# Attention with queries in blocks of 128, two heads sharing the last block, and half of the probabilities divided on GpSimd

## The chip, the cores and the metric

One Trainium2 chip, one of its cores. The time is the device time of one execution in microseconds; 853.25 us is the median of three runs of the kernel before. Engine names as in the profile: PE is TensorE's matmul, PEld its weight load, DVE is VectorE, ACT is ScalarE, POOL is GpSimd, SP is the engine that issues the transfers.

## What is computed

```python
def _attn_ref(q, k, v, g_q, g_k):            # 4 batches, 12 heads, 448 tokens, 64 wide
    q_n, k_n = (rmsnorm(q, g_q), rmsnorm(k, g_k))
    scores = scale * np.matmul(q_n, k_n.transpose(0, 1, 3, 2))
    scores = scores - np.max(scores, axis=-1, keepdims=True)
    attn = np.exp(scores)
    attn = attn / (np.sum(attn, axis=-1, keepdims=True) + 1e-09)
    return np.matmul(attn, v)
```

The result goes, as 1792 tokens of 768, through a gated MLP (`silu(x @ w_gate) * (x @ w_val) @ w_out`, width 1536), and that through a soft mixture of 8 experts with 4 slots each: logits by `phi`, a softmax over the tokens that makes the slots' inputs, two matmuls per expert with a ReLU between, and a softmax over the slots that mixes their outputs. All is fp32.

## The kernel before, in words

The work is one program with a list of steps written out by hand. A step `t` handles one block of 112 queries of one **pair** of heads; there are 24 pairs (6 per batch, `i` in the code) and 4 blocks per pair (`c`). Matmuls with fp32r operands are made exact enough by splitting an operand into a high and a low part.

- **Stage 0** (`step0`, steps 0 to 27, order lists `ORD0` and `ORDB`): attention of batch 0 and the start of batch 1, beside the conversion of the MLP's weights from 64-bit words and the product of `w_out` and `phi`.
- **Later steps** (`step`): each step also does one unit `u` of the gated MLP, `gv` (line 596), in two halves `G0` and `G1` of nine matmuls each (line 607). Attention of batch b+1 runs beside the MLP of batch b. `ORD1` (line 1244) is the order of a step while the weights are still converted (`u` < 24), `ORD2` (line 1247) the one after. Attention ends at step 95, near 610 us; the rest of the MLP, the slots and the experts follow, and the experts' weights are loaded as buffers come free.

Each name in an order list is a part of the step, issued in that order; each engine executes its instructions in that order, and waits where an operand or a buffer is late. The parts of attention, in the order of the data:

- `T`, `TH`, `L` (`transp` 365, `transp_hi` 390, `transp_lo` 410): transpose q or k of the next pair, then make the high and low parts. For pairs 0 to 6 (`SPL = 7`) both heads stand in the two halves of the partitions, one instruction per part. For later pairs each head's high and low parts are stacked: `qa[:, j]` holds the high part of head j in its own half of the partitions and the low part in the other half, and k's high part is copied into both halves, by ACT or DVE, so a full-height matmul covers two of the three terms.
- `S` (`scores` 448): pairs 0 to 6 take three terms x two heads, each a matmul with 64 contraction rows (line 463); later pairs take four matmuls of 128 rows (466 and 468).
- `M0`, `M1` (`smax` 471, DVE) and `E0`, `E1` (`sexp` 477, ACT): maximum and exponential of each head, with the row sums in `su`.
- `P0`, `P1` (`ptrans` 513, PE) and `V0`, `V1` (`pevac` 524, ACT or DVE), one step later: transpose the probabilities and copy them out of PSUM.
- `NA`, `NB`, `NC` (`sums_inv` 488, `sums_spread` 499, `sums_evac` 509): invert the eight columns of sums, widen them to 64 columns each on POOL (`rs`, line 494), transpose that on PE (`rb`, line 504) and copy it out, so that the sums lie along the queries.
- `X` (`pv` 538): 16 matmuls on v for the whole pair, into the PSUM tile `xp`; `XM` (`pv_scale` 567, DVE) multiplies by the inverse sums; `XH`, `XL` (`split_hi` 583, `split_lo` 587) make the parts of x.
- `Q` (`norm_part` 357): squares on ACT, and on POOL the power (line 341) and the products (347) of the RMS norm of a later pair.

PSUM: all transposes, `xp` and the small results share three buffers of one tag (`pt_tile`, line 67); the scores rotate over three more.

Of the kernel before, what the change touches and what calls it, by code (L numbers as in the profile page):

```python
# [8 lines left out]
F32 = mybir.dt.float32  # L9
# [12 lines left out]
def attn_moe_softmoe_kernel(  # L22
# [366 lines left out]

    def transp_hi(i, n):  # L390

        if i >= NPR:
            return
        tq = st[i]["qk"[n]]
        qa, ka, kl = qk_tiles(i)
        if i < SPL:
            if n == 0:
                nc.scalar.activation(out=qa[:, 0], in_=tq[:, :S], func=AF.Copy, scale=gsc[:, 0:1])
            else:
                (nc.vector.tensor_copy if i < NP and HID else nc.scalar.copy)(out=ka[:, 0], in_=tq[:, :S])  # L400
            return
        for j, r in enumerate(halves):
            if n == 0:
                nc.scalar.activation(out=qa[r, j], in_=tq[r, :S], func=AF.Copy, scale=gsc[r, 0:1])
            else:
                nc.scalar.copy(out=ka[r, j], in_=tq[r, :S])
                if (KC0 if i < NP else KC1)[j] == "a":
                    nc.scalar.copy(out=ka[halves[1 - j], j], in_=tq[r, :S])

    def transp_lo(i, n):  # L410

        if i >= NPR:
            return
        tq = st[i].pop("qk"[n])
        qa, ka, kl = qk_tiles(i)
        if i < SPL:
            if n == 0:
                nc.vector.scalar_tensor_tensor(
                    out=qa[:, 1],
                    in0=tq[:, :S],  # L420
                    scalar=gsc[:, 0:1],
                    in1=qa[:, 0].bitcast(F32),
                    op0=ALU.mult,
                    op1=ALU.subtract,
                )
            else:
                sub_lo(kl[:, 0], tq[:, :S], ka[:, 0])
            return
        for j, r in enumerate(halves):
            if n == 1 and i < SPL + 2:  # L430
                nc.gpsimd.memset(kl.bitcast(F32)[halves[1 - j], j], 0.0)
            o = halves[1 - j]
            if n == 0:
                nc.vector.scalar_tensor_tensor(  # L434
                    out=qa[o, j],
                    in0=tq[r, :S],
                    scalar=gsc[r, 0:1],
                    in1=qa[r, j].bitcast(F32),
                    op0=ALU.mult,
                    op1=ALU.subtract,  # L440
                )
            else:
                sub_lo(kl[r, j], tq[r, :S], ka[r, j])
                kc = (KC0 if i < NP else KC1)[j]
                if kc != "a":
                    (nc.gpsimd if kc == "p" else nc.vector).tensor_copy(out=ka[o, j], in_=ka[r, j])

    def scores(t):

        i, c = divmod(t, NC)  # L450
        d = st[i]
        qa, ka, kl = qk_tiles(i)
        if t < M0 and t % 2:
            sc = [ps.tile([P, S], F32, tag=g, name="s")[:CP] for g in "gv"]
        elif t < M0:
            sc = [s_tile(j)[:CP] for j in range(2)]
        else:
            sc = [s_tile((2 * (t - M0) + j) % 3)[:CP] for j in range(2)]
        cs = slice(c * CP, (c + 1) * CP)
        if i < SPL:  # L460
# [3 lines left out]
        else:  # L464
# [4 lines left out]
        d[c] = {"sc": sc, "sm": ap_.tile([CP, 2], F32, tag="sm", name="sm", bufs=4), "pr": {}}  # L469

    def smax(t, j):
        d = st[t // NC][t % NC]
# [4 lines left out]
    def sexp(t, j):  # L477
        i, c = divmod(t, NC)
        d = st[i][c]
        if "su" not in st[i]:  # L480
            st[i]["su"] = ap_.tile([CP, NC, 2], F32, tag="su", name="su", bufs=3)
        p = ap_.tile([CP, S], F32, tag="pr", name="pr", bufs=PRB)
# [3 lines left out]
        d["pr"][j] = p  # L486

    def sums_inv(i):

        su = st[i]["su"].rearrange("p c j -> p (c j)")  # L490
        nc.scalar.activation(out=su, in_=su, func=AF.Copy, bias=EPS_SUM)
        nc.vector.reciprocal(out=su, in_=su)  # L492
        rs = ap_.tile([P, 2 * NC * HD], F32, tag="rs", name="rs", bufs=1)
        nc.gpsimd.tensor_copy(  # L494
            out=rs[:CP].rearrange("p (n d) -> p n d", d=HD), in_=su.unsqueeze(2).to_broadcast([CP, 2 * NC, HD])
        )
        st[i]["rs"] = rs

    def sums_spread(i):

        rs = st[i]["rs"][:CP].rearrange("p (c n) -> p c n", c=NC)
        rb = pt_tile("rb")
        for c in range(NC):
            nc.tensor.transpose(
                rb[:, c * CP : (c + 1) * CP], rs[:, c], ident[:CP, :CP]
            )
        st[i]["rb"] = rb

    def sums_evac(i):
        st[i]["rs"] = st[i]["rs"][:, :S]  # L510
        nc.scalar.copy(out=st[i]["rs"], in_=st[i].pop("rb")[:, :S])

    def ptrans(t, j):

        i, c = divmod(t, NC)
        pr = st[i][c]["pr"][j]
        tp = pt_tile("tp")
        for ck in range(NC):
            nc.tensor.transpose(  # L519
                tp[:CP, ck * CP : (ck + 1) * CP], pr[:, ck * CP : (ck + 1) * CP], ident[:CP, :CP]  # L520
            )
        st[i][c]["tp", j] = tp

    def pevac(t, j):
        i, c = divmod(t, NC)
        if c == 0:
            if i < NP and i % 2:
                pt = hnp.tile([CP, NC, 512], F32, tag="hn", name="pt", bufs=3)[:, :, :S]
            else:
                pt = ap_.tile([CP, NC, S], F32, tag="pt", name="pt", bufs=PTB)  # L530
            st[i].setdefault("pt", {})[j] = pt
        eng = nc.vector.tensor_copy if t < M0 and (t % 4, j) in PVD else nc.scalar.copy
        eng(  # L533
            out=st[i]["pt"][j][:, :, c * CP : (c + 1) * CP],
            in_=st[i][c]["tp", j][:CP, :S].rearrange("p (k q) -> p k q", k=NC),
        )
# [98 lines left out]

    def h_trans(u, ht=None):

        b, r = divmod(u, NU)
        fc = r // 2
        g, f4 = divmod(fc, 4)  # L640
        d = bt[b]
        if f4 == 0:
            d["hn"][g] = hnp.tile([CP, NC, 512], F32, tag="hn", name="hn", bufs=3)
        ht = d["ht"][fc] if ht is None else ht
# [3 lines left out]
        nc.scalar.copy(  # L648
            out=d["hn"][g][:, :, P * f4 : P * f4 + P], in_=th4[:CP, :].rearrange("p (c f) -> p c f", c=NC)
        )  # L650
# [407 lines left out]
    def step(t):  # L1058
# [114 lines left out]

        def P_(j):
# [48 lines left out]
        def Q_():  # L1223
# [6 lines left out]
            SP=SP, R0=R0, R=R_, CT=CT, C=C_, SS=SS, HT=HT, LG=LG, Q=Q_,  # L1230
# [14 lines left out]
        "SP X NB T S AT W4 NC XM TH XH M1 M0 Z1 P1 Z2 WH AM G0 Z3 P0 E1 XL L NA R0 CT V0 V1 SS WL G1 E0 Q HT Z4 LG R C"  # L1245
# [9 lines left out]
    KC0, KC1 = 'aa', 'va'  # L1255
# [9 lines left out]
        "X TP WT P0 M1 NB M0 NA TH WV R SS TL S V0 U2 NC U W2 XM CT P1 C G2 WE V1 XH XL E0 Q E1"  # L1265
# [228 lines left out]
```

## Time and profile before

| what | value |
|---|---|
| median of three runs | 853.25 us (852.73 to 855.25) |
| the profiled execution | 852.55 us, of which the span from first to last instruction is 850.2 us |
| mean granted TensorE clock | 0.977 |
| busy: PE, DVE, ACT, POOL | 801.2, 492.1, 487.2, 270.0 us |
| DMA | 148.87 MB, mean 175 GB/s |
| chain that ended last, by engine | PE 76%, DVE 8%, DMA 7%, POOL 3%, ACT 3%, issue 2% |

A row of a group of instructions names the line, the engine, the operation, what it writes and from what (`out<-in`), the shapes, and the count. The chain follows the work that ended last back from the end, at each step to what released it. A wait row says who waited for whom, how long in all, how often and the longest.

### The profile page before, as it was taken

Reading aid. Unit: us, or ns where it says so; the run is one execution under the profiler, and the core shown is the slowest. Engines: PE = TensorE matmul, PEld = TensorE weight load, DVE = VectorE, ACT = ScalarE, POOL = GpSimd, SP = SyncE. Lnnn points to the kernel's source line nnn. Section 1 sums busy time; section 2 is a strip of 40 time slices with the busy share of each in tenths; the row PEclk is TensorE's granted clock in tenths of the full one; section 3 lists DMA queues with packets and bytes.
Section 4 is the critical chain, followed back from the end, with each engine's and each line's share of the span. In section 5 each row is a group of like instructions: output and inputs, shape, how many; then the busy total and the mean of one; then the engine's idle time right before and its main releaser. Section 6 shows DMA issues by size and latency. Waiting matters only on the chain.

```text
span 850.2 us, 14278 instructions
## 1 busy us (share of the span) xinstructions
PE 801.2 (94%) x5504; PEld 612.8 (72%) x5504; DVE 492.1 (58%) x785; ACT 487.2 (57%) x1054; POOL 270.0 (32%) x211
## 2 busy tenths in 40 slices
PE   6899989999999999999999999999999999988685
PEld 5566657878877767788778678877888888655343
DVE  4899888889888556565646655554354434221013
ACT  4777877889877746676667467664532323211012
POOL 7977748676777023113330230200000000010000
PEclk8999999999999999999999999999999999999877
DMA  7666655576564322322132122221227888799997
GB/s 212 201 178 205 205 179 185 178 248 198 186 196 152 108 60 66 107 89 89 51 94 89 49 78 67 86 67 57 59 77 239 294 293 319 271 383 403 403 350 235
DMA packets 77891, 148.87 MB, mean 175 GB/s; under 512 B 5888, under 2 KB 48128, under 8 KB 77824
## 3 DMA queue, kind: packets, MB, share of 16 engines
q1 hardware_dynamic: 77824, 147.97, 52.5%
q8 instruction: 43, 0.70, 0.3%
q14 instruction: 24, 0.20, 0.1%
HBM read 128.29 MB, written 19.66 MB: 174 GB/s over the span
## 4 chain that ended last, share of the span: by engine, by line
PE 76%; DVE 8%; DMA 7%; POOL 3%; ACT 3%; issue 2%; SPq 0%; POOLq 0%; ACTq 0%; DVEq 0%
PE pg L607 36%; PE tp L519 7%; PE xp L547 6%; DMA w<-in_moe_w_dram 6%; PE s L466 3%; PE s L468 3%; PE th L647 2%; PE tq L372 2%; DVE sm L473 2%; PE s L547 2%; DVE qa L434 2%; PE so L1436 2%; PE s L463 2%; PE lp L668 2%; POOL rs L494 2%
## 5 line engine op out<-in xcount | busy, mean ns | idle before, releaser
L607 PE MATMUL pg<-xh,wh 128*128 128x448 f32 x576 | 219.6, 381 | 0.0
L607 PE MATMUL pg<-xl,wh 128*128 128x448 f32 x576 | 210.3, 365 | 0.0
L607 PE MATMUL pg<-xh,wl 128*128 128x448 f32 x432 | 158.1, 366 | 0.7 <-DVE wl L239 0.7
L473 DVE TENSOR_REDUCE sm<-s 112x1 f32<-112x448 f32 x192 | 110.7, 618 | 66.6 <-PE s L468 65.3
L483 ACT ACTIVATE pr<-s,sm 112x448 f32<-112x448 f32 x192 | 121.1, 635 | 37.5 <-DVE sm L473 36.3
L494 POOL COPY rs<-su 112x512 f32<-112x512 f32 x24 | 35.6, 1484 | 275.1 <-DVE su L492 268.2
L607 PEld LDWEIGHTS pg<-xh,wh 128*128 128x128 f32 x576 | 108.4, 188 | 17.9 <-issue 10.2
L607 PEld LDWEIGHTS pg<-xl,wh 128*128 128x128 f32 x576 | 108.6, 189 | 7.0
L519 PE MATMUL tp<-ident,pr 112*112 112x112 f32 x768 | 99.6, 261 | 3.0 <-ACT wot L253 1.1
L519 PEld LDWEIGHTS tp<-ident,pr 112*112 112x112 f32 x768 | 82.2, 134 | 17.9 <-issue 2.1
L231 ACT CAST wh<-raw 128x768 fp32r<-128x768 f32 x96 | 79.7, 831 | 25.2 <-PE pg L607 21.8
L533 ACT COPY pt<-tp 112x448 f32<-112x448 f32 x164 | 81.0, 539 | 13.8 <-PE tp L519 7.8
L607 PEld LDWEIGHTS pg<-xh,wl 128*128 128x128 f32 x432 | 81.1, 188 | 8.5 <-DVE wl L239 2.0
L239 DVE TENSOR_TENSOR wl<-raw,wh 128x768 fp32r<-128x768 f32 x72 | 72.7, 1009 | 23.4 <-ACT wh L231 23.1
L341 POOL TENSOR_TENSOR ri<-ss,mhalf 112x16 f32<-112x16 f32 (+1 forms) x25 | 70.2, 2806 | 2.1
L347 POOL TENSOR_TENSOR qn<-qk,ri 112x512 f32<-112x512 f32 x46 | 62.1, 1361 | 2.3
L621 ACT ACTIVATE ht<-pg 128x448 f32<-128x448 f32 x48 | 25.9, 539 | 56.3 <-PE pg L607 56.3
L547 PE MATMUL xp<-pt,vt 112*64 112x448 f32 x288 | 58.1, 545 | 0.0
L648 ACT COPY hn<-th 112x512 f32<-112x512 f32 x48 | 28.4, 592 | 46.6 <-PE th L647 45.2
L607 PE MATMUL pg<-xh,raw 128*128 128x448 f32 x144 | 52.7, 366 | 0.0
L197 POOL TENSOR_SCALAR hpos<-r 128x768 uint16<-128x768 int16 x36 | 44.6, 1239 | 12.2 <-DVE raw L212 8.8
L628 DVE SCALAR_TENSOR_TENSOR ht<-ht,pg 128x448 f32<-128x448 f32 x48 | 29.5, 614 | 31.9 <-ACT ht L621 31.3
(160 smaller groups left out, 1208.7 us busy)
## 6 DMA issues: line engine op xcount, KB each, us to landing
w<-in_moe_w_dram SPq DMA_DIRECT2D x25, 1536.0 KB, 10.3
raw<-w SPq DMA_DIRECT2D x72, 384.0 KB, 3.1
w<-raw SPq DMA_DIRECT2D x36, 384.0 KB, 3.0
r<-in_moe_w_out_dram SPq DMA_DIRECT2D x12, 768.0 KB, 5.2
r<-in_moe_w_gate_dram SPq DMA_DIRECT2D x12, 768.0 KB, 5.7
r<-in_moe_w_val_dram SPq DMA_DIRECT2D x12, 768.0 KB, 5.3
qk<-in_q_dram SPq DMA_DIRECT2D x24, 224.0 KB, 3.4
qk<-in_k_dram SPq DMA_DIRECT2D x24, 224.0 KB, 3.5
```

The costliest lines, as they stand in the source:

```text
L197: (nc.gpsimd if e == "p" else nc.vector).tensor_scalar(out=o, in0=src, scalar1=-float((0x3800, 0xB800)[j]), scalar2=8.0, op0=ALU.add, op1= ...
L231: (nc.vector.tensor_copy if u - NO < NU and WH1 == "v" else nc.scalar.copy)(out=wh, in_=wst[u]["raw"])
L239: eng.tensor_tensor(out=wl, in0=wst[u]["raw"], in1=wst[u]["wh"].bitcast(F32), op=ALU.subtract)
L341: nc.gpsimd.tensor_tensor(out=ri, in0=ss, in1=mhalf[:, : len(ns)], op=ALU.pow)
L347: eng.tensor_tensor(out=st[i]["qn"][:, n].rearrange("p c h d -> p h c d"), in0=st[i]["qk"][:, n], in1=st[i]["ri"][:, n] .rearrange("p (h c ...
L473: nc.vector.tensor_reduce(out=d["sm"][:, j : j + 1], in_=d["sc"][j], axis=AX.X, op=ALU.max, negate=True)
L483: nc.scalar.activation(out=p, in_=d["sc"][j], func=AF.Exp, bias=d["sm"][:, j : j + 1], accum_out=st[i]["su"][:, c, j : j + 1])
L494: nc.gpsimd.tensor_copy(out=rs[:CP].rearrange("p (n d) -> p n d", d=HD), in_=su.unsqueeze(2).to_broadcast([CP, 2 * NC, HD]))
L519: nc.tensor.transpose(tp[:CP, ck * CP : (ck + 1) * CP], pr[:, ck * CP : (ck + 1) * CP], ident[:CP, :CP])
L533: eng(out=st[i]["pt"][j][:, :, c * CP : (c + 1) * CP], in_=st[i][c]["tp", j][:CP, :S].rearrange("p (k q) -> p k q", k=NC),)
L547: nc.tensor.matmul(xp[HD * j : HD * j + HD, :S], d["vt"][:, j, ck, :], d["pt"][j][:, ck, :], start=(ck == 0), stop=(ck == NC - 1),)
L607: nc.tensor.matmul(d[r], wt[:, P * c : P * c + P], mv, start=(c == 0 and n == 0), stop=(c == KD - 1 and n == 2),)
```

## The change

Queries are cut into three blocks of 128 and one of 64 per head. The last 64 queries of both heads of a pair share one block: a tile `qz`, zeroed once, holds head 0's 64 queries in its half of the partitions and columns 0 to 63, head 1's in the other half and columns 64 to 127, so one full-height matmul gives the scores of both. All pairs now use the three-term form of the scores; the stacked form and its copies of k go. In batches 2 and 3 (pairs 12 to 23) the probabilities are divided by their sums on POOL before they are transposed, so the spreading of the sums and the multiplication of the output go there; the split of x reads PSUM. Blocks per pair stay four, the last with one tile of scores instead of two. The three order lists are rearranged.

```diff
+    QL = S % P
+    qz = [ap_.tile([P, 2, 2 * QL], F32R, name=f"qz{n}") for n in range(2)]
...
     def transp_lo(i, n):
...
+            for j, r in enumerate(halves):
+                nc.gpsimd.tensor_copy(out=qz[i % 2][r, :, QL * j : QL * j + QL], in_=qa[r, :, S - QL :])
+        else:
+            sub_lo(ka[:, 1], tq[:, :S], ka[:, 0])
...
     def scores(t):
-        if i < SPL:
-            for n, (wt, mv) in enumerate(((qa[:, 0], ka[:, 0]), (qa[:, 0], kl[:, 0]), (qa[:, 1], ka[:, 0]))):
+        terms = ((0, 0), (0, 1), (1, 0))
+        for n, (wt, mv) in enumerate(terms):
+            if c < NC - 1:
                 for j, r in enumerate(halves):
-                    nc.tensor.matmul(sc[j], wt[r, cs], mv[r, :], start=(n == 0), stop=(n == 2))
-        else:
-            for j in range(2):
-                nc.tensor.matmul(sc[j], qa[:, j, cs], ka[:, j], start=True, stop=False)
-            for j in range(2):
-                nc.tensor.matmul(sc[j], qa[:, j, cs], kl[:, j], start=False, stop=True)
+                    nc.tensor.matmul(
+                        sc[j], qa[r, wt, c * P : (c + 1) * P], ka[r, mv, :], start=(n == 0), stop=(n == 2)
+                    )
+            else:
+                nc.tensor.matmul(sc[0], qz[i % 2][:, wt], ka[:, mv], start=(n == 0), stop=(n == 2))
...
+    def normp(t, part):
+        i, c = divmod(t, NC)
+        if part > both(t):
+            return
+        su = st[i]["su"][:, c, : both(t)]
+        if part == 0:
+            nc.vector.tensor_scalar(out=su, in0=su, scalar1=EPS_SUM, scalar2=None, op0=ALU.add)
+            nc.vector.reciprocal(out=su, in_=su)
+        else:
+            j = part - 1
+            p = st[i][c]["pr"][j]
+            nc.gpsimd.tensor_scalar(out=p, in0=p, scalar1=su[:, j : j + 1], scalar2=1.0, op0=ALU.mult, op1=ALU.mult)
...
     def pevac(t, j):
...
+        if c < NC - 1:
+            eng(out=st[i]["pt"][j][:, :, c * P : (c + 1) * P], in_=tp)
+        else:
+            eng(out=st[i]["pt"][j][:, :, c * P :], in_=tp[:, :, QL * j : QL * j + QL])
...
     def pv_scale(i):
+        if i >= NPX:
+            xt[b, hp] = d["xp"][:, :S]
...
-        "AT NB X NC T S XM TH XH M0 M1 AM XL E0 E1 SP W4 G0 L NA Z1 Z3 WH P0 V0 P1 V1 Z2 Z4 HT LG SS R0 CT C WL G1 R Q"
+        "T S AT TH M0 Z3 NB X NC P0 AM XM XH W4 M1 XL SP CT E0 SS NA G0 E1 Z1 WH V0 N0 Z4 P1 Q HT L R0 N2 V1 N1 C Z2 WL R G1 LG"
```

`both(t)` is 1 for the last block of a pair and 2 otherwise. `NPX` is 12. `N0` is the sum and reciprocal, `N1` and `N2` are the multiplications of heads 0 and 1.

## Rows read from the trace of the kernel before

**Rows 1.** The page, part 1: busy time, share of the span, instructions.

```profile
PE 801.2 (94%) x5504; PEld 612.8 (72%) x5504; DVE 492.1 (58%) x785; ACT 487.2 (57%) x1054; POOL 270.0 (32%) x211
```

**Rows 2.** Stretches: length, busy time per engine (instructions), PE clock, DMA share, GB/s.

```profile
145.00:238.00 93.00, 93.00 (x558) 76.82 (x557) 78.97 (x109) 80.30 (x160) 65.64 (x39) 1.00 0.67 210
...
270.00:330.00 60.00, 56.95 (x341) 43.85 (x340) 37.04 (x58) 35.86 (x80) 13.10 (x10) 1.00 0.24 76
...
500.00:610.00 110.00, 108.84 (x640) 89.48 (x640) 56.74 (x91) 67.15 (x152) 16.36 (x13) 1.00 0.22 68
...
770.00:790.00 20.00, 17.30 (x346) 11.09 (x342) 0.77 (x6) 1.15 (x3) 0.94 (x3) 1.00 1.03 402
```

**Rows 3.** Chain of waits, one pair of batch 2: start, length, what.

```profile
530.24 0.39 PE rb L504 x4
530.63 3.16 PE xp L547 x16
...
542.23 0.77 PE tp L519 x8
543.00 0.44 PE th L647 x4
...
545.27 0.40 PE s L466 x2
545.67 0.40 PE s L468 x2
546.07 1.85 PE pg L607 x9
...
554.80 0.62 PE th L647 x4
...
557.25 0.39 PE rb L504 x4
```

**Rows 4.** Timeline of PE, one step of stage 0: start, length, what.

```profile
74.04 0.55 PE L519 MATMUL tp<-ident,pr 112*112 112x112 f32 x4
74.52 0.46 PE L463 MATMUL s<-ka,qa 64*112 64x448 f32 x2
74.81 0.36 PE L463 MATMUL s<-kl,qa 64*112 64x448 f32 x2
75.02 0.37 PE L463 MATMUL s<-ka,qa 64*112 64x448 f32 x2
75.31 0.41 PE L274 MATMUL wpq<-stack,wot 128*128 128x32 f32 x2
```

**Rows 5.** Waits of PE: for whom, us in total, times, longest.

```profile
PE th L647 <- DVE qa L434: 4.7, 10, 0.5
...
PE rb L504 <- POOL rs L494: 2.1, 1, 2.1
```

**Rows 6.** Timeline of ACT, one exponential of batch 2.

```profile
541.51 0.63 ACT L483 ACTIVATE pr<-s,sm 112x448 f32<-112x448 f32 x1
542.03 0.20 ACT L483 ACTIVATION_READ_ACCUMULATOR pr<-s,sm 112x1 f32 x1
```

**Rows 7.** Timeline of DVE in batch 2.

```profile
540.23 1.16 DVE L473 TENSOR_REDUCE sm<-s 112x1 f32<-112x448 f32 x2 [0.47 <-PE s L468]
541.30 0.61 DVE L634 SCALAR_TENSOR_TENSOR ht<-ht,pg 128x448 f32<-128x448 f32 x1
542.99 0.96 DVE L239 TENSOR_TENSOR wl<-raw,wh 128x768 fp32r<-128x768 f32 x1 [1.07 <-ACT wh L231]
...
554.68 0.20 DVE L492 RECIPROCAL su<-su 112x8 f32<-112x8 f32 x1
```

**Rows 8.** Timeline of POOL in batch 2.

```profile
499.61 2.29 POOL L494 COPY rs<-su 112x512 f32<-112x512 f32 x1 [25.04 <-DVE su L492]
...
502.27 2.90 POOL L341 TENSOR_TENSOR ri<-ss,mhalf 112x16 f32<-112x16 f32 x1
...
526.92 0.61 POOL L494 COPY rs<-su 112x512 f32<-112x512 f32 x1 [19.62 <-DVE su L492]
```

More of the change, by code (lines that the diff above doesn't have):

```diff
@@ L375, in transp, with qz_zeros @@
         st[i][nm] = tq
-    SPL = 7
+    NPX = 2 * NP
     halves = [slice(0, HD), slice(HD, P)]
-    klz = [ap_.tile([P, 2, S], F32R, name=f"kl{n}") for n in range(2)]
+    QL = S % P
+    qz = [ap_.tile([P, 2, 2 * QL], F32R, name=f"qz{n}") for n in range(2)]
+    def qz_zeros():
+        for n in range(2):
+            nc.vector.memset(qz[n].bitcast(F32), 0.0)
     def qk_tiles(i):
@@ L394, in transp_hi @@
         tq = st[i]["qk"[n]]
-        qa, ka, kl = qk_tiles(i)
-        if i < SPL:
-            if n == 0:
-                nc.scalar.activation(out=qa[:, 0], in_=tq[:, :S], func=AF.Copy, scale=gsc[:, 0:1])
-            else:
[L400 to L408, printed above, removed]
+        qa, ka = qk_tiles(i)
+        if n == 0:
+            nc.scalar.activation(out=qa[:, 0], in_=tq[:, :S], func=AF.Copy, scale=gsc[:, 0:1])
+        else:
+            (nc.vector.tensor_copy if i < NP and HID else nc.scalar.copy)(out=ka[:, 0], in_=tq[:, :S])
     def transp_lo(i, n):
@@ L414, in transp_lo @@
         tq = st[i].pop("qk"[n])
[L415 to L446, printed above, removed]
+        qa, ka = qk_tiles(i)
+        if n == 0:
+            nc.vector.scalar_tensor_tensor(
+                out=qa[:, 1],
+                in0=tq[:, :S],
+                scalar=gsc[:, 0:1],
+                in1=qa[:, 0].bitcast(F32),
+                op0=ALU.mult,
+                op1=ALU.subtract,
+            )
[3 more added lines that the diff above has]
+            sub_lo(ka[:, 1], tq[:, :S], ka[:, 0])
     def scores(t):
@@ L477, in sexp @@
     def sexp(t, j):
+        if j >= both(t):
+            return
         i, c = divmod(t, NC)
@@ L499, in sums_spread @@
     def sums_spread(i):
-        rs = st[i]["rs"][:CP].rearrange("p (c n) -> p c n", c=NC)
         rb = pt_tile("rb")
         for c in range(NC):
-            nc.tensor.transpose(
-                rb[:, c * CP : (c + 1) * CP], rs[:, c], ident[:CP, :CP]
-            )
+            cs = slice(c * P, (c + 1) * P)
+            nc.tensor.transpose(rb[:, cs], st[i]["rs"][:, cs], ident)
         st[i]["rb"] = rb
     def sums_evac(i):
-        st[i]["rs"] = st[i]["rs"][:, :S]
-        nc.scalar.copy(out=st[i]["rs"], in_=st[i].pop("rb")[:, :S])
+        rs = st[i]["rs"] = st[i]["rs"][:, :S]
+        rb = st[i].pop("rb")
+        n = S - QL
+        nc.scalar.copy(out=rs[:, :n], in_=rb[:, :n])
+        for j, r in enumerate(halves):
+            nc.scalar.copy(out=rs[r, n:], in_=rb[r, n + QL * j : n + QL * j + QL])
     def ptrans(t, j):
+        if j >= both(t):
+            return
         i, c = divmod(t, NC)
@@ L518, in ptrans @@
         for ck in range(NC):
[L519 to L521 removed]
+            nc.tensor.transpose(tp[:CP, ck * P : (ck + 1) * P], pr[:, ck * CP : (ck + 1) * CP], ident)
         st[i][c]["tp", j] = tp
@@ L570, in pv_scale @@
         d = st.pop(i)
+        if i >= NPX:
+            xt[b, hp] = d["xp"][:, :S]
+            if b == 3 and hp > 3:
+                xf = xfp.tile([P, S], F32, tag=f"xh{hp - 4}", name="xf", bufs=1)
+                nc.scalar.copy(out=xf, in_=xt[b, hp])
+                xt[b, hp] = xf
+            return
         if b == 3 and hp > 3:
@@ L647, in h_trans @@
             nc.tensor.transpose(th4[:CP, P * c : P * c + P], ht[:, CP * c : CP * c + CP], ident)
-        nc.scalar.copy(
-            out=d["hn"][g][:, :, P * f4 : P * f4 + P], in_=th4[:CP, :].rearrange("p (c f) -> p c f", c=NC)
-        )
+        nc.scalar.copy(out=hn[:, :, o : o + P], in_=th4[:CP, :].rearrange("p (c f) -> p c f", c=NC))
     def logits(u):
@@ L1172, in E_, with NP_ @@
                 sexp(t, j)
+        def NP_(part):
+            if att and i >= NPX:
+                normp(t, part)
         def P_(j):
@@ L1273, in attn_moe_softmoe_kernel @@
         setup()
+        qz_zeros()
         fill(16)
```

68 lines of the change are left out of this document (36 added, 32 removed).

## The prediction

> **What bounds the kernel now.** I read the busy shares first: TensorE (PE) is busy 94% of the span, VectorE and ScalarE under 60% [rows 1]. Shares mix stages, so the stretches come next [rows 2]. From 145 to 238 us, where attention of batch 1 runs beside the MoE of batch 0, PE is busy all 93 us. From 500 to 610 us, where attention of batches 2 and 3 runs beside the MoE of batches 1 and 2, it misses 1.2 of 110 us. It misses 3.05 us in 270 to 330. In the tail (770 to 790 us) PE is busy 17.3 of 20 us, but the DMA share is full at 402 GB/s: the expert weights bound it. Those loads are issued by steps and as buffers come free, so the tail starts earlier by as much as PE ends the stages before it earlier. A microsecond of PE's queue before 610 us is therefore a microsecond of the kernel; one of ScalarE or VectorE is worth what PE waits for it.
>
> The chain of waits shows one pair of heads in that stage, as pieces one after the other with no gap [rows 3]: from one group rb (530.24) to the next (557.25) is 27.01 us. Per block of queries it holds the scores, 0.40 + 0.41 us, and eight transposes of probabilities, 0.77 us; per pair once rb, 0.39 us, and the 16 matmuls on v, 3.16 us.
>
> **The change, part by part.** Pairs 0 to 6 have K=64 scores now, 7 to 23 stacked ones; pairs 12 to 23 lose the spreading of the sums.
>
> *Scores, blocks 0 to 2.* Pairs 7 to 23 go from four full-height matmuls (0.81 us) to six of half height. Pairs 0 to 6 show what those cost [rows 4]: the two halves run at once, since the groups of two start 0.20 to 0.30 us apart; from the transposes at 74.04 to the group behind at 75.31 is 1.27 us. Less four transposes (0.77 / 8 each, 0.385) that is 0.885 us, more than three times 0.20, the rest being lost at the two changes of shape. So +0.075 us x 3 blocks x 17 pairs = +3.8 us. Bounds: 0.61 us (no loss at the changes, -10.2 us) to 1.16 us (twice the loss, +17.9).
>
> *Scores, fourth block.* Both heads share three full-height matmuls, 0.61 us by 0.81 / 4: -0.20 x 17 = -3.4 us, and against 0.885 us in pairs 0 to 6, -0.27 x 7 = -1.9 us.
>
> *Transposes of probabilities.* 32 of 112 columns become 28 of 128. Four of 112 take 0.385 us, four of 128 take 0.44 us (th) [rows 3]: 8 x 0.385 = 3.08 against 7 x 0.44 = 3.08 us. Nothing. Pairs 0 to 11 still spread their sums, now with 128 columns: 12 x 0.05 = +0.6 us.
>
> *Sums of batches 2 and 3.* rb goes: 12 x 0.39 = -4.7 us. Its copy on ScalarE, the wide copy on GpSimd and the multiplication of the output go too; PE hid them, so nothing, except that PE waited once for the GpSimd copy, 2.1 us [rows 5]: -2.1 us.
>
> *A wait that goes.* PE waited ten times, 4.7 us in all, before th for VectorE's qa [rows 5]; the row at 554.80 is one, th drawn out to 0.62 us behind it [rows 3]. Two low parts of q, one per head, hold a PSUM slot of the three that all transposes share. The new code has one instruction there, and in that step the block before is a fourth one with a single group of transposes, so a slot is free: -4.7 us. Next late would be the second group of transposes in the step of the output, which needs the slot of xp or of the first group.
>
> *Division on GpSimd.* Per block it adds two small VectorE instructions and one or two GpSimd multiplications of 128x448 between the exponential and PE's transposes, one step later. The trace of before has no such multiplication. Lower bound: GpSimd's copy of 512 columns at 0.61 us [rows 8] scaled to 448, 0.53 us. Upper bound: the same copy at 2.29 us, when something held it. I take 0.6, as a one-input pass over SBUF is nearest to the copy. The tightest place is block 2. From its scores' start: scores 0.885; two maxima and the activation's product between them, 1.16 + 0.61 [rows 7], to 2.65; last exponential and its accumulator read, 0.63 + 0.20 [rows 6], to 3.5; sum and reciprocal at 0.20 each [rows 7], to 3.9; two multiplications to 5.1 us. PE comes to the first transpose after 0.885 + 0.44 + 1.85 + 0.44 + 0.44 + 1.85 + 0.61 = 6.5 us. 1.4 us are spare. After block 1 PE has the 3.16 us on v too, but the exponentials now stand behind the split of x; about 1.6 us are spare. After block 0 the next step's matmuls on v cover it; block 3 has one multiplication. Before its multiplications GpSimd has the power, 2.90 us once per pair [rows 8], which fits since rb's copy is gone. Cost nothing; without that cover two multiplications cost their excess over 2.6 us, 12 times each in two places.
>
> The Trainium skill speaks against this placement: GPSIMD Engine Reference, section Engine selection, gives elementwise work to VectorE, GpSimd being about twice slower with two inputs and near line rate with one. Twice VectorE's 0.61 us [rows 7] would be an estimate of 1.2 us each, the chain then ends at 6.3 us, and the sum stays; it leaves 0.2 us of cover. No row here shows this operation.
>
> *The rest.* ScalarE and VectorE lose an exponential, a maximum and the doubled copies of k per pair; that work was hidden, but some of the 3.05 us in 270 to 330 [rows 2] are waits for it: -1 us taken, 0 to -3 the bounds. The zeroing of two tiles at the start, two small GpSimd copies per pair and two more ScalarE copies in pairs 0 to 11 are small beside idle time: nothing; uncovered they would cost about a microsecond. Reordered lists move instructions inside a step, not PE's sum; if they uncover a wait, that is the first rival.
>
> Sum: +3.8 - 3.4 - 1.9 + 0.6 - 4.7 - 2.1 - 4.7 - 1 = -13.4 us. The profiled execution took 852.55 us (span 850.2), 0.7 below the median 853.25: 839.1 for it, 839.8 for a median; I write 839.5.
>
> **Rivals.**
>
> *A, the waits only move.* xp now stays in PSUM until both halves of x are split from it, in a step where three other groups want the three slots. For it: one wait of this sort exists, 0.47 us a time. Against: PE has 1.85 us of MoE before it needs the slot. Then the 4.7 + 2.1 + 1 us stay: 853.25 - 5.6 = 847.5.
>
> *B, GpSimd ends on the path, slower.* The place is the first transpose after blocks 1 and 2; it decides from 1.3 us per multiplication, and the kernel is slower than before from about 1.7. For it: the same copy took 0.61 and 2.29 us, and VectorE's wl of 0.96 us [rows 7] stands beside the multiplications in each step. At 2.0 us each, 1.4 + 1.2 us per pair are lost, 12 x 2.6 = 31: 870. Against: 1.4 us spare, and one wl can add 0.96 to the pair only once. The lock behind this is told in the Trainium skill, SBUF — State Buffer, section SBUF: two separate sides: GpSimd and a VectorE instruction with two SBUF inputs exclude each other for a whole instruction. The two durations of the copy fit it.
>
> *C, half-height scores cost more between MoE groups.* At the upper bound, 1.16 us, they cost +17.9 instead of +3.8: 853.5, no change. For it: nobody ran them in that stage. Against: the neighbours in rows 4 change shape just as often.
>
> **How the numbers follow.** Forecast 0.57, A 0.20, B 0.13, C 0.10. The range reaches down to 831 (scores at 0.70 us, all of the idle time gone) and up to 852, taking in A and part of C; B lies outside. About 0.3% (2.6 us) is what a measurement can tell from no change. Faster: forecast, A and the mild end of B, 0.80; same 0.09; slower 0.11.
>
> **What would show it.** Right: X to X about 26 us in batch 2; no rb after batch 1; PE's wait for qa gone; half-height scores near 0.885 us in the MoE stage; GpSimd's multiplications near 0.6 us with no PE wait on them; the tail as long as before. Wrong: PE waiting for GpSimd's pr, multiplications over 1.3 us, score groups over 1.1 us, or new waits in 100 to 330 us, where ScalarE and VectorE are fullest.

## The result, and the profile after

The kernel after takes 839.3 us (median of 4 runs, 838.59 to 839.75), the kernel before 853.92 in the runs beside it (852.73 to 855.25): ratio 0.9836, 95% interval 0.9813 to 0.9859. The prediction said 839.5. The total is right; two of its parts are wrong, by 8.3 and 6.3 us, in opposite directions.

The page, part 1 (busy time, share of the span, instructions) and two of its costliest groups, of the kernel after:

```profile
span 837.7 us, 14201 instructions
PE 794.4 (95%) x5424; PEld 596.0 (71%) x5424; DVE 464.6 (55%) x796; ACT 440.9 (53%) x957; POOL 333.1 (40%) x327
...
L486 POOL TENSOR_SCALAR pr<-pr,su 128x448 f32<-128x448 f32 x84 | 70.2, 847 | 117.3 <-DVE su L482 106.3
...
L423 POOL CAST qz<-qa 64x128 fp32r<-64x128 f32 x48 | 33.7, 703 | 83.4 <-DVE qa L414 75.1
```

The span is 12.5 us shorter than before [rows 1]. To see where, I set both traces on the same marks: the group of 16 matmuls on v (xp; "X" below), once per pair, from pair 6 on. X of pair 6 stands at 129.27 before and at 136.08 after; X of pair 22 at 584.83 and at 573.83.

- **Up to the first X: 6.8 us lost.** The prediction had about 1.5 gained there (1.9 less some of the 0.6 for rb).
- **From X of pair 6 to X of pair 22: 455.56 becomes 437.75, 17.8 us gained.** The prediction's terms for these 16 pairs make 11.5.
- **From there to the end: 265.4 becomes 263.9**, about what the last pair gains.

The stretches between these two X of the kernel before, cut at the pairs with the longer steps, two of the six with the sum of all (columns as in [rows 2]):

```profile
129.27:273.18 143.91, 141.13 (x835) 115.21 (x834) 120.51 (x167) 119.41 (x236) 104.72 (x63) 1.00 0.62 196
...
330.36:469.05 138.69, 136.10 (x805) 111.59 (x804) 80.81 (x128) 93.41 (x205) 33.43 (x25) 1.00 0.27 82
...
sum 455.56, PE 444.68 PEld 359.19 DVE 300.11 ACT 320.52 POOL 169.38; mean PE 74.11 PEld 59.86 DVE 50.02 ACT 53.42 POOL 28.23
```

The same stretches of the kernel after:

```profile
136.08:278.21 142.13, 141.50 (x843) 112.03 (x842) 107.35 (x155) 107.36 (x222) 96.11 (x70) 1.00 0.62 199
...
331.19:463.98 132.79, 132.79 (x791) 104.43 (x789) 76.11 (x138) 79.64 (x170) 61.45 (x68) 1.00 0.28 88
...
sum 437.75, PE 437.11 PEld 340.86 DVE 275.55 ACT 279.15 POOL 221.17; mean PE 72.85 PEld 56.81 DVE 45.92 ACT 46.53 POOL 36.86
```

PE was idle for 455.56 - 444.68 = 10.9 us between the marks before, and is idle for 0.6 after; its busy time fell by 7.6. So 10.2 us of the 17.8 are waits and 7.6 are work.

The chain of waits of the kernel after, from X of pair 20 to X of pair 21 (start, length, what), answers to [rows 3]:

```profile
521.75 3.16 PE xp L552 x16
524.90 0.58 PE tp L525 x4
525.48 1.84 PE pg L619 x9
...
529.59 0.81 PE s L442 x5
530.40 0.58 PE tp L525 x4
530.98 1.84 PE pg L619 x9
532.83 0.44 PE tp L525 x4
533.26 0.44 PE th L663 x4
...
535.52 0.60 PE s L446 x3
536.12 0.44 PE tp L525 x4
...
546.94 0.80 PE s L442 x6
547.74 3.16 PE xp L552 x16
```

X to X is 25.99 us, against 27.00 for the same two pairs before; the other pairs from 13 to 22 gain 1.0 to 1.4 us each, the one with longer steps (18 to 19) 2.75. A half-height block takes 0.80 or 0.81 us, as the full-height one did, and the transposes right behind take 0.58 instead of 0.44; where the matmuls on v stand right behind (547.74), nothing is added. The fourth block takes 0.60. There is no rb and no idle time.

The wait before th is gone, and one more look at the step of the fourth block's transposes shows why (PE, VectorE and ScalarE of the kernel after):

```profile
544.12 0.60 PE L663 MATMUL th<-ident,ht 128*112 128x128 f32 x4
544.73 0.67 DVE L414 SCALAR_TENSOR_TENSOR qa<-tq,gsc,qa 128x448 fp32r<-128x448 f32 x1
545.03 0.37 ACT L541 COPY pt<-tp 112x256 f32<-112x256 f32 x1
```

th starts before VectorE reads q's transpose (tq) for its low part and before ScalarE copies the block's one group of transposes (tp), so it has a slot that neither of them holds.

Three losses at the start show in PE's timeline (in brackets the idle time before, and for whom), of the kernel after:

```profile
18.44 1.01 PE L372 MATMUL tq<-ident,qn 112*128 112x112 f32 x4 [4.63 <-POOL qn L347]
...
44.17 0.88 PE L506 MATMUL rb<-ident,rs 128*128 128x128 f32 x4 [1.74 <-POOL rs L496]
44.97 1.49 PE L442 MATMUL s<-ka,qa 64*128 64x448 f32 x6
...
113.14 0.87 PE L247 MATMUL tw<-ident,raw 128*128 128x128 f32 x3 [2.67 <-DVE raw L212]
```

Before, the first of these waits took 2.18 us and the other two weren't there. For the first, POOL's own timeline, of the kernel before:

```profile
11.96 0.21 POOL L340 TENSOR_SCALAR ss<-ss 112x16 f32<-112x16 f32 x1 [2.45 <-DVE ss L327]
```

and of the kernel after:

```profile
13.34 0.64 POOL L423 CAST qz<-qa 64x128 fp32r<-64x128 f32 x2 [3.97 <-DVE qa L414]
14.07 0.21 POOL L340 TENSOR_SCALAR ss<-ss 112x16 f32<-112x16 f32 x1
```

The two small copies of pair 0's last columns of q take 0.64 us, but they wait until 13.34 for VectorE's low part of q, and the normalization of pair 1 stands behind them in POOL's queue: 2.1 us late. PE waits for it.

For the third, VectorE's timeline of the kernel after:

```profile
111.70 0.42 DVE L541 COPY pt<-tp 112x256 f32<-112x256 f32 x1 [2.00 <-ACT pt L541]
```

This is the copy of head 1's half of the fourth block, out of the one tile of transposes that both heads share. It waits 2.00 us until ScalarE has copied head 0's half, which stands in ScalarE's queue behind a pass of 1.19 us over the weights; raw, which PE waits for, stands behind it in VectorE's queue. That the shared tile makes one copy wait for the other is read from the code, not tested.

### The profile page after: what moved, and what is told of

The parts are those of the page before. It is cut to its first block, busy times and chain, and to the rows that moved or that the text cites. A ratio compares the mean times of both kernels' runs of the same rounds, so it can differ in the third digit from the quotient of the medians.

```text
span 837.7 us, 14201 instructions
## 1 busy us (share of the span) xinstructions
PE 794.4 (95%) x5424; PEld 596.0 (71%) x5424; DVE 464.6 (55%) x796; ACT 440.9 (53%) x957; POOL 333.1 (40%) x327
## 4 chain that ended last, share of the span: by engine, by line
PE 61%; DMA 4%; ACT 1%; DVE 1%; POOL 1%; SPq 0%; issue 0%; DVEq 0%; ACTq 0%; POOLq 0%
PE pg L619 33%; PE tp L525 5%; PE xp L552 5%; DMA w<-in_moe_w_dram 4%; PE s L442 3%; PE so L1456 3%; PE th L663 2%; PE sp L750 1%; PE lp L683 1%; PE s L1429 1%; PE tq L372 1%; PE s L446 1%; PE s L1415 1%; PE sip L804 0%; PE ln L707 0%; PE warm_ps L115 0%
## 5 line engine op out<-in xcount | busy, mean ns | idle before, releaser
L457 DVE TENSOR_REDUCE sm<-s 128x1 f32<-128x448 f32 x168 | 100.8, 619 | 74.9 <-PE s L442 52.2
L469 ACT ACTIVATE pr<-s,sm 128x448 f32<-128x448 f32 x168 | 106.2, 639 | 59.1 <-DVE sm L457 58.8
L619 PEld LDWEIGHTS pg<-xh,wh 128*128 128x128 f32 x576 | 108.4, 188 | 12.5 <-issue 5.1
L486 POOL TENSOR_SCALAR pr<-pr,su 128x448 f32<-128x448 f32 x84 | 70.2, 847 | 117.3 <-DVE su L482 106.3
L525 PE MATMUL tp<-ident,pr 128*112 128x128 f32 x672 | 102.9, 281 | 2.6 <-ACT pr L469 1.4
L525 PEld LDWEIGHTS tp<-ident,pr 128*112 128x112 f32 x672 | 75.2, 136 | 37.4 <-issue 13.7
L231 ACT CAST wh<-raw 128x768 fp32r<-128x768 f32 x96 | 79.5, 830 | 28.2 <-PE pg L619 22.8
L239 DVE TENSOR_TENSOR wl<-raw,wh 128x768 fp32r<-128x768 f32 x72 | 78.5, 1090 | 11.2 <-ACT wh L231 11.2
L539 ACT COPY pt<-tp 112x512 f32<-112x512 f32 x123 | 70.1, 594 | 20.1 <-PE tp L525 11.9
L423 POOL CAST qz<-qa 64x128 fp32r<-64x128 f32 x48 | 33.7, 703 | 83.4 <-DVE qa L414 75.1
L442 PE MATMUL s<-ka,qa 64*128 64x448 f32 x432 | 65.8, 410 | 0.8 <-ACT qa L403 0.7
L347 POOL TENSOR_TENSOR qn<-qk,ri 112x512 f32<-112x512 f32 x46 | 54.0, 1174 | 1.1
```

The lines of the kernel that those rows point to most:

```text
L231: (nc.vector.tensor_copy if u - NO < NU and WH1 == "v" else nc.scalar.copy)(out=wh, in_=wst[u]["raw"])
L239: eng.tensor_tensor(out=wl, in0=wst[u]["raw"], in1=wst[u]["wh"].bitcast(F32), op=ALU.subtract)
L347: eng.tensor_tensor(out=st[i]["qn"][:, n].rearrange("p c h d -> p h c d"), in0=st[i]["qk"][:, n], in1=st[i]["ri"][:, n] .rearrange("p (h c ...
L442: nc.tensor.matmul(sc[j], qa[r, wt, c * P : (c + 1) * P], ka[r, mv, :], start=(n == 0), stop=(n == 2))
L457: nc.vector.tensor_reduce(out=d["sm"][:, j : j + 1], in_=d["sc"][j], axis=AX.X, op=ALU.max, negate=True)
L469: nc.scalar.activation(out=p, in_=d["sc"][j], func=AF.Exp, bias=d["sm"][:, j : j + 1], accum_out=st[i]["su"][:, c, j : j + 1])
```

## The experiments

Each is compared with runs of the kernel before on its chip. "Between the marks" is from X of pair 6 to X of pair 22.

**1. The small copies behind the powers of pair 1.** The kernel after, with pair 0's copies moved down GpSimd's queue:

```diff
+    def qz_fill(i):
+        qa, ka = qk_tiles(i)
+        for j, r in enumerate(halves):
+            nc.gpsimd.tensor_copy(out=qz[i % 2][r, :, QL * j : QL * j + QL], in_=qa[r, :, S - QL :])
...
-            for j, r in enumerate(halves):
-                nc.gpsimd.tensor_copy(out=qz[i % 2][r, :, QL * j : QL * j + QL], in_=qa[r, :, S - QL :])
+            if i > 0:
+                qz_fill(i)
...
+        qz_fill(0)
```

> The changed kernel, with the two GpSimd copies into qz for pair 0 issued behind the power and the products of pair 1's norm instead of ahead of them. Theory (the copies stand in GpSimd's queue ahead of the power that PE waits for in the prologue, 4.63 us against 2.18 before): PE's wait falls back to about 2.2 us and the whole kernel gains 2 to 3 us, about 837 us. Rival (the prologue's delay is taken up later in stage 0, which is bound by something else): PE's wait shortens, but the time stays within 1 us of the changed kernel's 839.3.

838.01 us (ratio 0.9832, 0.9799 to 0.9865); first X at 133.13, between the marks 437.70. GpSimd starts on pair 1's sums at 11.86 again. PE's waits, of this kernel:

```profile
PE tq L372 <- POOL qn L347: 3.3, 2, 1.7
```

(us in total, times, longest: 4.6 was the longest after.) So the queue order is the cause of this wait's growth. The time alone cannot show it, its interval covers that of the kernel after.

**2. The order of the first stage's steps from before.**

```diff
     ORD0 = (
-        "M1 M0 X TP P0 R WT NA NB TH SS S U2 TL V0 WV NC W2 U P1 XM CT C WE E0 V1 E1 XH Q XL G2"
+        "X TP WT P0 M1 NB M0 NA TH WV R SS TL S V0 U2 NC U W2 XM CT P1 C G2 WE V1 XH XL E0 Q E1"
```

> The changed kernel with the list ORD0 of the kernel before (its names are the same), so that the widening of the sums stands ahead of the weights' GpSimd pass again. Theory (the new list lets rb wait 1.74 us for GpSimd at 44 us, after which PE runs at a lower clock for some us, and tw wait 2.67 us at 113 us): both waits go, 3 to 5 us gained, 835 us. Rival (the new list suits the new blocks, and the waits come from the added GpSimd copies): no gain, or 1 to 3 us lost.

837.31 us (ratio 0.9816, 0.9778 to 0.9853); first X at 132.84, between the marks 437.74. PE's wait of 1.74 us for the spread sums (rs) is gone: in the new list GpSimd reaches R, which issues passes of 1.07 us each to its queue, ahead of NA, whose copy of the sums PE waits for. The wait of 4.6 us for qn is still there. So is the third wait, which the expectation put down to the list too:

```profile
110.03 0.87 PE L247 MATMUL tw<-ident,raw 128*128 128x128 f32 x3 [2.67 <-DVE raw L212]
```

It stands, with 2.67 or 2.68 us, in every kernel that has the new blocks (experiments 1 to 3 and 5 to 10), under either list, and neither in the kernel before nor in experiment 4. So it comes with the new blocks and not with this list; no run takes it away. The time, as in experiment 1, cannot show the gain.

Both first X are compared with 136.08, which turned out to be the latest of six: the kernels of experiments 3, 5, 6, 7 and 8 have the same first stage as after, and their first X stand at 134.69, 134.49, 133.25, 134.56 and 134.54. Against 134.5, the usual one, the two repairs are worth 1.4 and 1.7 us, as an estimate: each is one trace, and the six of the same stage lie from 133.25 to 136.08, so neither alone (133.13, 132.84) is clear of them. What is shown for each alone is its wait. What sets 136.08 apart stands in the last section.

**3. All sums spread.** The kernel after with no division of probabilities:

```diff
-    NPX = 2 * NP
+    NPX = NPR
```

> The changed kernel with NPX = 24: no division on GpSimd, the sums of all pairs spread by PE as in batches 0 and 1; the new blocks, scores and lists stay. Theory (the division is worth the rb groups, 12 x 0.4 to 0.5, plus one wait of PE for the wide copy): 5 to 8 us slower than the changed kernel, 844 to 847. Rival (the division is worth most of the gain because it also frees PSUM slots, ScalarE and VectorE): 12 us or more slower, 851 or above. Second rival (GpSimd's multiplications cost as much as they save): within 1 us of 839.3.

845.08 us (ratio 0.9904, 0.987 to 0.9938). The stretch between the marks, of this kernel:

```profile
134.69:578.92 444.23, 443.83 (x2660) 345.61 (x2659) 265.80 (x406) 289.27 (x633) 164.83 (x138) 1.00 0.37 118
```

PE is idle for 0.4 us: the waits are gone without the division. They go with the blocks and the list together (experiment 8 parts the two). The division is worth 444.23 - 437.75 = 6.5 us, which is the group rb, 0.59 us here, in 11 pairs.

**4. Division alone.** The kernel before (blocks of 112, stacked scores, its lists) with the division on GpSimd in pairs 12 to 23, put into its lists behind the exponentials:

```diff
+    NPX = 2 * NP
...
-            if c == 0 and NP < i <= NPR:
+            if c == 0 and NP < i <= NPX:
...
     ORD2 = (
-        "AT NB X NC T S XM TH XH M0 M1 AM XL E0 E1 SP W4 G0 L NA Z1 Z3 WH P0 V0 P1 V1 Z2 Z4 HT LG SS R0 CT C WL G1 R Q"
+        "AT NB X NC T S XM TH XH M0 M1 AM XL E0 E1 SP W4 G0 L N0 NA Z1 Z3 WH P0 V0 P1 V1 N2 N1 Z2 Z4 HT LG SS R0 CT C WL G1 R Q"
```

> The kernel before with nothing changed but the division of batches 2 and 3 on GpSimd (blocks of 112, stacked scores and the old lists stay; sum, reciprocal and multiplications put behind the exponentials). Theory (parts add up): 5 to 8 us faster than before, 846 to 849, and PE still waits some 4 to 5 us for qa ahead of th. Rival (the division needs the new lists or the three larger blocks, with eight multiplications per pair instead of seven): no gain, PE waits for GpSimd's pr.

850.11 us (ratio 0.9968, 0.9951 to 0.9985). The stretch between the marks and PE's longest entry of waits in it, of this kernel:

```profile
129.81:584.52 454.71, 442.99 (x2593) 355.25 (x2592) 308.50 (x522) 314.09 (x659) 227.71 (x189) 1.00 0.36 114
```

```profile
PE th L667 <- ACT pt L546: 5.2, 10, 0.7
```

Division alone takes 0.9 us off the stretch. rb is gone, but PE is idle for 11.7 us. The wait before th, ten times 4.7 us in all before [rows 5], is still there ten times, 5.2 us; only the name behind it has changed, from VectorE's qa to ScalarE's copy of the transposed probabilities. The slot that th needs is held by another reader. VectorE still has its two low parts of q there. So the waits only move, as in rival A of the prediction, though in a kernel with blocks of 112 and not by xp, which rival A had. The 0.9 us is a balance: the pair with which the division begins (X of pair 11 to X of pair 12) takes 26.68 us instead of 24.07, with more waits and with the granted clock at 0.50 for 3.4 us from 280.4; the ten pairs behind it gain 2.6 us together, 0.26 each, where rb was 0.39. The parts do not add: blocks and lists alone give 455.56 - 444.23 = 11.3, division alone 0.9, both 17.8.

**5 and 6. Two and three multiplications.** The kernel after, with one or two more passes over the same tile by 1.0, which leave the result as it is (the diff of three; two has one of the lines):

```diff
             nc.gpsimd.tensor_scalar(out=p, in0=p, scalar1=su[:, j : j + 1], scalar2=1.0, op0=ALU.mult, op1=ALU.mult)
+            nc.gpsimd.tensor_scalar(out=p, in0=p, scalar1=1.0, scalar2=1.0, op0=ALU.mult, op1=ALU.mult)
+            nc.gpsimd.tensor_scalar(out=p, in0=p, scalar1=1.0, scalar2=1.0, op0=ALU.mult, op1=ALU.mult)
```

> The kernel after, with each division on GpSimd followed by two more multiplications of the same tile by 1.0 (the result is the same). One multiplication took 0.64 us (median), so three take about 1.92. Rival B of the prediction: the place decides from 1.3 us per multiplication, two of them cost their excess over 2.6 us at two places of each of 12 pairs, 2 x 1.92 - 2.6 = 1.24, times 24 = 30 us: about 869 us against 839.3, with PE waiting for pr at the first transpose behind blocks 1 and 2. Other theory, that the new list of the MoE stage issues the multiplications so early that far more than 1.4 us is spare: under 3 us longer, and PE's waits for pr under 5 us in all.

> The kernel after, with each division on GpSimd followed by one more multiplication of the same tile by 1.0 (the result is the same). In the kernel with three, the first took 0.64 us and each further one 0.57, so two take 1.21 each block half, under the 1.3 from which the prediction says that GpSimd decides: first theory, under 3 us longer than 839.3 and PE's waits for pr under 3 us in all. Rival, that the power and the products of the normalization, which stand in the same queue, have used up the rest: PE waits for pr as often as with three (17 times, 22.4 us), the time lies halfway to 868.6, about 854.

Three: 868.62 us (ratio 1.0182, 1.016 to 1.0204). Two: 845.54 us (ratio 0.9918, 0.9885 to 0.995). PE's waits between 270 and 640 us with three, and with two:

```profile
PE tp L527 <- POOL pr L488: 22.4, 17, 3.2
```

```profile
PE tp L526 <- POOL pr L487: 6.2, 13, 1.9
```

With three, one division is 0.642 + 2 x 0.566 = 1.774 us by medians (not 1.92, as expected). By these, two exceed 2.6 us by 0.95, 24 times 22.8, near the 22.4 us of the waits, but this agreement is luck: the waits are 17 and not 24, one place of a pair (behind block 1) loses 1.4 to 2.0 us, the other (behind block 2) 0.2 to 0.4, and medians hide what happens in these places. GpSimd and VectorE behind block 2 of one pair of the kernel after:

```profile
533.49 1.96 POOL L486 TENSOR_SCALAR pr<-pr,su 128x448 f32<-128x448 f32 x2 [3.20 <-DVE su L482]
533.64 1.29 DVE L239 TENSOR_TENSOR wl<-raw,wh 128x768 fp32r<-128x768 f32 x1 [0.35 <-ACT wh L231]
```

The first multiplication takes 0.64 us, the second, beside VectorE's wl, 1.34. Of the 84, 21 take 1.17 to 1.35 us, all of them beside a wl; the mean is 0.85 (the page above). The two end at 535.45 and PE's timeline has its first transpose of them at 535.95: 0.5 us are spare, not 1.4. The chain at the same place with two passes:

```profile
538.75 0.65 POOL pr L486
539.47 1.15 POOL pr L487
540.62 0.63 POOL pr L486
541.32 0.57 POOL pr L487
```

Two divisions take 3.00 us here, not 2 x 1.20. That is 0.40 more than 2.6; PE waits 0.38 us, and 0.33 to 0.40 behind block 2 in nine pairs. So the 2.6 us that the prediction worked out for this place hold. Neither theory of the second expectation does: the time grew by 6.2 us, the waits are 6.2 in 13 places. At the one multiplication of the change PE waited for it once, 0.6 us, at the first pair that is divided.

**7. Division on VectorE.**

```diff
-            nc.gpsimd.tensor_scalar(out=p, in0=p, scalar1=su[:, j : j + 1], scalar2=1.0, op0=ALU.mult, op1=ALU.mult)
+            nc.vector.tensor_scalar(out=p, in0=p, scalar1=su[:, j : j + 1], scalar2=1.0, op0=ALU.mult, op1=ALU.mult)
```

> The kernel after, with the division of the probabilities on VectorE instead of GpSimd, at the same places of the list. VectorE's pass over such a tile took 0.61 us, GpSimd's 0.64 (median) and 2.24 at most. Theory 1, VectorE has the room (busy 53% of 500 to 597 us): the same time within 2 us, X to X in batch 2 about 26.0 us. Theory 2, the place matters: 7 x 0.61 = 4.3 us per pair stand in VectorE's list ahead of the next maxima and of the evacuations, PE then waits for VectorE's maxima or low parts: over 4 us longer, X to X above 26.4.

837.71 us (ratio 0.981, 0.9788 to 0.9833), between the marks 437.22. One tile of the probabilities in that kernel (min/median/max of a duration in ns, first and last start), then in the kernel after:

```profile
L486 DVE TENSOR_SCALAR pr<-pr,su x84: 438/448/1249, 268.7 to 588.1; 128x448 f32<-128x448 f32 x84
```

```profile
L486 POOL TENSOR_SCALAR pr<-pr,su x84: 637/642/2243, 270.6 to 590.3; 128x448 f32<-128x448 f32 x84
```

VectorE needs 0.45 us for it, GpSimd 0.64. The rule that the prediction weighed (the Trainium skill, GPSIMD Engine Reference, section Engine selection) has the right direction; for this one-input pass the ratio is 1.43 by the medians, more than the near line rate that the section gives for one input and less than the factor of about two that it gives for two. But both are hidden, and the 0.5 us between the marks is all that the time can show. Theory 1 holds.

**8. The order of the MoE stage's steps from before**, with the new sums and divisions put in:

```diff
     ORD2 = (
-        "T S AT TH M0 Z3 NB X NC P0 AM XM XH W4 M1 XL SP CT E0 SS NA G0 E1 Z1 WH V0 N0 Z4 P1 Q HT L R0 N2 V1 N1 C Z2 WL R G1 LG"
+        "AT NB X NC T S XM TH XH M0 M1 AM XL E0 E1 SP W4 G0 L N0 NA Z1 Z3 WH P0 V0 P1 V1 N2 N1 Z2 Z4 HT LG SS R0 CT C WL G1 R Q"
```

> The kernel after, with the order of the MoE stage's steps from before (the sums and divisions put in behind the places that need them). From the first X (pair 6) to that of pair 22 the kernel after takes 437.75 us, before 455.56. Theory of the prediction, the wait before th goes because the fourth block leaves a slot free, whatever the list: about 438 again, no wait of th. Rival, the new list is what removes it, as division alone with the old list kept the wait (ten times, 5.2 us): waits of 4 to 6 us come back, 442 to 445.

844.77 us (ratio 0.9891, 0.9859 to 0.9924). The sum between the marks, and a part of the chain in one pair, of this kernel:

```profile
sum 442.73, PE 441.36 PEld 341.77 DVE 270.18 ACT 278.10 POOL 226.17; mean PE 73.56 PEld 56.96 DVE 45.03 ACT 46.35 POOL 37.70
```

```profile
527.53 0.80 PE s L442 x4
528.33 2.04 PE pg L619 x9
530.37 0.98 PE tp L525 x8
531.35 1.82 PE pg L619 x9
```

Both theories are half right. The time between the marks is the rival's (442.73, 5.0 us more than after), the reason is not: PE is idle for 1.4 us only and no wait of th came back, so the wait goes with the blocks, whatever the list, as the prediction said. What the list changes is PE's busy time, 441.36 against 437.11. In the old list the MoE group of nine stands right behind the half-height scores and takes 2.04 us instead of 1.84; the new list puts transposes there (0.58 instead of 0.44), or the matmuls on v (nothing added). The pair that takes 25.99 us after takes 26.39 here. A change of shape costs 0.20, 0.14 or nothing, by what stands behind it.

**9 and 10. The repairs together.** Nine is one and two in one kernel. Ten adds the division on VectorE, and puts the small copies of pairs 0 and 1 there:

```diff
-            nc.gpsimd.tensor_copy(out=qz[i % 2][r, :, QL * j : QL * j + QL], in_=qa[r, :, S - QL :])
+            (nc.vector if i < 2 else nc.gpsimd).tensor_copy(out=qz[i % 2][r, :, QL * j : QL * j + QL], in_=qa[r, :, S - QL :])
...
-            nc.gpsimd.tensor_scalar(out=p, in0=p, scalar1=su[:, j : j + 1], scalar2=1.0, op0=ALU.mult, op1=ALU.mult)
+            nc.vector.tensor_scalar(out=p, in0=p, scalar1=su[:, j : j + 1], scalar2=1.0, op0=ALU.mult, op1=ALU.mult)
```

> The kernel after with the first two repairs together: pair 0's two small GpSimd copies issued behind the powers of pair 1, and the order of the first stage's steps from before. Alone they took 2.95 and 3.24 us off the time of the first X (136.08). If the two losses stand at different places they add: first X near 129.9, 833.1 us, faster than after by 6. If the second only makes up for what the first did, first X near 132.8 and 836.5 us.

> Both repairs together with the division on VectorE, and the small copies of q's last columns on VectorE too in pairs 0 and 1. If GpSimd's queue is what is left of the loss in the first stage, PE's wait of 1.04 us for the spread sums goes and the first X comes at about 130 (131.07 with both repairs alone); with the 0.5 us that division on VectorE took off the stage from there (437.22 against 437.75) the time is 831.0 against 832.6. If VectorE, the fullest engine there beside PE, becomes late instead, the first X comes at 132 or later: 833.5 or more.

Nine: 832.64 us (831.94 to 834.64; ratio 0.9758, 0.9739 to 0.9777), first X at 131.07, between the marks 437.74. Ten: 832.68 us (831.31 to 834.3; ratio 0.977, 0.9744 to 0.9795), first X at 129.95, between the marks 437.22. Both first X lie below all six of the unrepaired stage (133.25 to 136.08); against the usual 134.5 nine takes off 3.4 us, about 1.4 + 1.7, so the losses do stand at different places. In ten PE's wait of 1.04 us for the spread sums is gone and the first X comes 1.1 us earlier, as its first theory had it; the 831.0 us expected did not come. Behind X of pair 22 ten took 263.7 us in its profiled run and nine 262.0. Both are faster than before and after, by intervals that do not meet that of the kernel after. The profiled run of nine is 6.8 us shorter than that of after, 5.0 of it up to the first X and 1.8 behind X of pair 22, where nothing was edited (experiments 1 and 2, with the same code there, took 263.8 and 263.7); that part stays open.

What is left of the loss up to the first X is, on balance, the third wait. In ten PE is idle for 15.5 us up to there and busy for 114.4, in the kernel before 12.8 and 116.5: 2.7 us more idle time, the size of that wait, and 2.0 less work, where the prediction had 1.5.

## Why the prediction was right, and where it was wrong

**Scores, blocks 0 to 2: right.** 0.80 to 0.81 us, with 0.14 on the transposes behind in two of three blocks: 3 x 0.805 + 2 x 0.14 = 2.70 us per pair against 2.43 before, +0.27 where the sum had +0.225. Rival C fell; in the old list a block would cost 0.81 + 0.20, between the forecast and that rival.

**Fourth block, transposes, rb: right.** 0.60 for 0.81 us; seven groups of 0.44 for eight of 0.385; rb, 0.39 us, gone. The division is worth 6.5 us in the new kernel, where rb would have cost 0.59 (experiment 3), and 0.9 in the old one, where the wait before th stayed and the first divided pair lost 2.6 us (experiment 4).

**The wait before th: the mechanism right, the size too small.** It went with the fourth block's free slot: it stayed in experiment 4, which has blocks of 112, and was gone in 3 and 8, which have the new ones; that th had a slot of its own is read from the trace of the kernel after (544.12). The waits of the sum, 4.7 + 2.1 + 1 = 7.8 us, measured 10.2: others between the marks went too, such as one of 1.3 us for ScalarE's pr and those for VectorE's kl and ce, 0.2 to 0.5 us each, and behind a wait PE's next group is drawn out (th 0.62 us instead of 0.44 [rows 3]), which is in its busy time.

**The lists at nothing: wrong, twice.** "Reordered lists move instructions inside a step, not PE's sum" is a step that failed. The list of the MoE stage took 5.0 us off (experiment 8), 4.25 of it from PE's busy time, since it decides which shapes are neighbours. The list of the first stage put 1 us passes ahead of the copy that PE waits for and cost about 1.7 us (experiment 2, an estimate). The prediction had only waits in mind, and looked for new ones in 100 to 330 us, while two of the three lie ahead of 50.

**A new wait in 100 to 330 us: this sign of being wrong came.** The 2.67 us before tw, at 113.14, are in no term of the sum. The prediction counted the fourth block's gain in scores and transposes, not that VectorE's copy out of it can wait for ScalarE's.

**The small GpSimd copies at nothing: wrong.** "Small beside idle time" is a step that failed. They take 1.4 us per pair on average (33.7 us in 24 pairs), 0.64 for pair 0; uncovered was not their length but their wait. With the prediction's own question (what stands behind the waiting instruction in its queue) the answer was in the code: the power of the next pair. 2.1 us on GpSimd, about 1.4 of them in the time of the first X (experiment 1, an estimate).

**GpSimd's multiplications: covered, as forecast, with less to spare.** The median is 0.64 us for the 0.6 taken, but one of two stands beside wl and takes 1.34: 0.5 us are spare behind block 2 where the prediction had 1.4. It had named wl under rival B, and left it out of the cover. Its longer copy, 2.29 us from 499.61 [rows 8], stays unexplained: wl starts there only at 500.48, when a copy of 0.61 us would have ended. The place from which GpSimd decides is as forecast, 2.6 us for two (experiment 5); rival B would have come true with slower multiplications (experiment 6: PE waits 22.4 us), though not as its sum has it, with the same loss in both places.

So the terms of the steady pairs were sound: 27.00 - 25.99 = 1.01 us per pair, of which the sum had 0.84. That the total came out within 0.2 us is luck: between the marks 6.3 us more came off than the terms make (4.25 of PE's work by the list and 2.4 of extra waits, neither foreseen), and they roughly cancel the 8.3 us of error at the start.

## What to carry to other kernels

When PE is the bound, count the neighbours of a group as well as its matmuls: in the same kernel the same half-height scores cost 0.20, 0.14 or no extra time by what was issued behind them, and an order of steps that looks neutral moved 5 us. A small instruction on an idle engine is free only if nothing urgent is queued behind what it waits for. And when a wait on a shared PSUM slot is priced, count the slots: with blocks of 112 the reader named last changed from VectorE to ScalarE and the wait stayed, and with a slot free it went under either list.

## What was not expected of the hardware

**The clock after a wait.** The granted clock of PE fell around waits at the start. Stretches of the kernel after (columns as in [rows 2], the clock is the third figure from the end):

```profile
18.40:22.00 3.60, 3.56 (x16) 2.70 (x17) 1.78 (x3) 2.03 (x6) 3.39 (x4) 0.50 0.44 150
113.00:120.00 7.00, 6.86 (x35) 4.33 (x37) 3.79 (x6) 2.41 (x7) 5.87 (x3) 0.53 0.57 169
44.10:46.40 2.30, 2.23 (x12) 1.32 (x12) 0.00 (x0) 1.23 (x4) 2.14 (x4) 0.58 0.45 180
```

0.50 is the lower level (1.2 GHz). PE had waited 4.63, 2.67 and 1.74 us right before; in the first case the clock was down as that wait began (1.00 in 12.6 to 13.6 us, 0.50 from 13.8), behind three shorter ones of 0.7 to 1.2 us. A group of scores of half height then takes 1.49 us instead of 0.87. In 113 to 120 us the kernel before, without the wait before tw, has 1.00. The kernel of experiment 7, with the same instructions there and a similar wait for rs, kept 1.00 in 45 to 50 us: whether the clock falls behind a wait of that size differs from run to run, and this one drop is most of the 1.5 us between the first X at 136.08 and the usual 134.5. In experiment 6 it makes some of the long waits dearer. Two stretches of that kernel, each right behind a wait of PE for pr, of 2.01 and of 1.99 us:

```profile
405.80:409.00 3.20, 3.15 (x22) 2.98 (x22) 1.60 (x3) 1.73 (x4) 2.69 (x3) 1.00 0.00 0
463.40:466.40 3.00, 2.97 (x10) 2.74 (x11) 1.59 (x3) 1.76 (x4) 2.49 (x3) 0.50 0.00 0
```

PE's timeline in that kernel, a third of these waits and the transposes behind it:

```profile
524.86 1.10 PE L527 MATMUL tp<-ident,pr 128*112 128x128 f32 x4 [2.01 <-POOL pr L488]
```

At the lower level the transposes take 1.10 us, where those at 405.85 take 0.65, and the group of nine behind them takes 2.94 us in the chain instead of 1.84. The stretch between the marks is 30.0 us longer than after (467.73 against 437.75): PE is idle for 20.3 us more and busy for 9.7 more, 7.9 of these in the four pairs in which the clock fell. A wait of the same size brought the fall in one pair and not in another; what decides it, these runs don't show.
